# Weight conversion through one PSUM bank, and attention products issued straight behind the scores

## The chip, the cores and the metric

One core of one Trainium2 chip runs the whole program. The metric is the device time of one execution in microseconds (us), as the median of several. Five engines work side by side, each through its own instruction stream in order: TensorE (PE in the profile, its weight loads PEld), VectorE (DVE), ScalarE (ACT), GpSimd (POOL), and SyncE (SP), which issues the DMAs. They meet only at semaphores.

## The reference

Two layers follow each other. The first is attention with 8 batches, 8 heads, 576 positions and head size 64, in which each row of scores keeps only its 32 largest:

```
scores = q @ k.T / 8
kth    = 32nd largest of each row
scores = where(scores >= kth, scores, -1e9)
attn   = exp(scores - max); attn = attn / (sum + 1e-9)
x      = attn @ v                       # heads side by side: 576 x 512 for each batch
```

The second is a gated feed-forward layer with d_ff = 1024:

```
h    = relu(x @ w_in)                   # 576 x 1024
conv = cw[0]*h[s-1] + cw[1]*h[s] + cw[2]*h[s+1]
out  = (h * sigmoid(conv)) @ w_out      # 576 x 512
```

The weights `w_in`, `conv_w` and `w_out` arrive as 64-bit floats. [...]

## The kernel before

**Attention.** Two heads form a pair (`pc`); a batch has four pairs, and the program has 32 of them in order. The rows of a pair are cut into 9 tiles, j = 0 to 8: for j = 0 to 7 an even and the odd tile behind it are 128 query rows of the one head and of the other, and j = 8 holds the last 64 rows of both. That makes 288 tiles. `iteration(it)` runs once for each, and in every iteration each engine gets the work of several tiles that stand at different stages:

- PE (line order in the iteration): four transposes of the weighted row e of a tile (L306, into the bank `pt`), a budget of feed-forward matmuls (`run_units`, L804: expand L404 into `me`, contract L554 into `mc`), the transpose of the tail (L319), the scores of a new tile pair (`scores`, L811, only in iterations whose new tile has an even j), and the attention product (`av`, L813) of an earlier pair.
- ACT: the sign of each score against the threshold (L268), the copy of a score tile out of PSUM (`evacuate`, L228), the copy of the transposes (L311), the copy of a finished product (`av_out`, L348), the exponential of a tile (L280), and then tanh (L465), relu (L418), casts (L531) and tail copies (L323) of the feed-forward part.
- DVE: seven partial top-8 (L235) woven with their merges (L255, L257), `below` (L283), `select` (L287, called hot in the profile), the gates of the feed-forward layer (L473), and last `weigh` (L293), which multiplies the exponential with the mask.
- POOL: the weight conversion's arithmetic, the convolution, and `flip` (L273).

For PE, DVE, ACT and POOL the order is the order in which this code issues the instructions; no scheduler moves them. `weigh` needs the exponential of the iteration before, the next exponential overwrites its only buffer and so waits for `weigh`, and the transposes of the next iteration need its result.

**PSUM.** The scores lie in one tile of three banks, `s_ps`. An even tile is read from columns 0 to 575 (bank 0 and the start of bank 1), an odd one from 960 to 1535 (the end of bank 1 and bank 2). The two scores matmuls (L219, 64 rows of the array each) fill banks 0 and 2; a third with all 128 rows (`ends`, L222) fills the two 64-column pieces at the edges of bank 1. The attention product writes to the middle of the same bank 1 (`corner`, L121). Dependencies between engines are kept by bank, so whoever reads or writes any column of bank 1 waits for whoever used that bank on another engine before.

**When the attention product comes.** The pair whose second tile is transposed in one iteration is put on a list, and `av` runs in the next. That next iteration has an odd new tile, and so no scores. Its result is copied by L348 one iteration later, which is one with scores.

**Weight conversion.** 33 blocks (one of 24 columns, then 32 of 128 x 256) are converted, one per iteration: seven while the pipeline fills, before the first `weigh`, and then one in each of the next 26 iterations. One block takes three DVE instructions: L150 cuts the 16-bit exponent field out of the raw words, L151 the high mantissa, L161 puts the sign into the power. ACT makes the power from the field (L155) and two floats from the mantissa words (L156, L157); POOL multiplies and splits (L166 to L172). All these operands lie in SBUF. The feed-forward layer of a batch starts when its attention is done.

Of the kernel before, what the change touches and what calls it, by code (L numbers as in the profile page):

```python
# [13 lines left out]
BF16 = mybir.dt.bfloat16  # L14
U16 = mybir.dt.uint16
# [48 lines left out]
def attend_and_feed(ctx: ExitStack, tc: tile.TileContext, q, k, v, weights, out, shared, finish=None):  # L64
# [53 lines left out]
    def bank(name):  # L118
        return ps.tile([P, BANK], F32, name=name, tag=name, bufs=1)
# [6 lines left out]
    class Convert:  # L126
# [5 lines left out]
        def load(self):  # L132
            i = Convert.count
            Convert.count += 1
            if not scratch:
                scratch.append(moe.tile([P, 4 * SPB, WB], F32, name="scratch", tag="split"))
            self.at = i % SPB * 4
            tag = ("x_hi", "x_lo")[i % 2]
            self.raw = xp.tile([P, self.src.shape[-1], 2], U32, name="raw64", tag=tag)[0:self.n]
            nc.sync.dma_start(out=self.raw.rearrange("a c t -> a (c t)"), in_=self.src.bitcast(U32))  # L140
# [2 lines left out]
            return scratch[0][0:self.n, self.at + i, 0:self.raw.shape[1]]  # L143

        def split(self):
            exponent, self.mantissa, self.rest = (self.tmp(i) for i in range(3))
            n = exponent.shape[1]
            self.field, self.power = exponent.bitcast(U16)[:, 0:n], exponent.bitcast(BF16)[:, n:2 * n]
            self.top = self.raw.rearrange("a c t -> a (c t)").bitcast(U16).rearrange("a (c t) -> a c t", t=4)[:, :, 3]
            yield lambda: nc.vector.tensor_scalar(self.field, self.top, 0x7FF0, None, ALU.bitwise_and)  # L150
            yield lambda: nc.vector.tensor_scalar(self.mantissa.bitcast(U32), self.raw[:, :, 1], 0xFFFFF, 0x100000,  # L151
                                                  ALU.bitwise_and, ALU.bitwise_or)

        def act(self):
            nc.scalar.activation(out=self.power, in_=self.field, func=AF.Exp, scale=math.log(2.0) / 16, bias=offset)  # L155
            nc.scalar.activation(out=self.mantissa, in_=self.mantissa.bitcast(U32), func=AF.Copy, scale=2.0 ** -20)  # L156
            nc.scalar.activation(out=self.rest, in_=self.raw[:, :, 0], func=AF.Copy, scale=2.0 ** -52)  # L157

        def sign(self):
            power = self.power.bitcast(U16)  # L160
            yield lambda: nc.vector.scalar_tensor_tensor(out=power, in0=self.top, scalar=0x8000, in1=power,  # L161
                                                         op0=ALU.bitwise_and, op1=ALU.bitwise_or)

        def pool(self):
            x = self.mantissa
# [40 lines left out]
    def scores(t):  # L206
        kx, qx = t.pc.nat["k"], t.pc.nat["q"]
        i = t.j // 2
        rows_of = [slice(h * D, (h + 1) * D) for h in range(2)]
        if t.j == 2 * NI:  # L210
            for to, n in ((0, MAIN), (MAIN, TAIL)):
                for h, d in enumerate(rows_of):
                    at = (to + TAIL * h) % S
                    nc.tensor.matmul(s_ps[rows_of[1 - h], to:to + n], lhsT=qx[d, 0:TAIL], rhs=kx[d, at:at + n],  # L214
                                     start=True, stop=True)
        elif t.j % 2 == 0:
            at = slice(TAIL + i * P, TAIL + (i + 1) * P)
            for h, d in enumerate(rows_of):
                nc.tensor.matmul(s_ps[:, 2 * h * BANK:(2 * h + 1) * BANK], lhsT=qx[d, at],  # L219
                                 rhs=kx[d, h * TAIL:h * TAIL + MAIN], start=True, stop=True)  # L220
            ends = s_ps[:, BANK:2 * BANK].rearrange("p (a c) -> p a c", c=TAIL)[:, 0:BANK // TAIL:BANK // TAIL - 1]
            nc.tensor.matmul(ends, lhsT=qx[:, at], rhs=kx[:, S:S + 2 * TAIL], start=True, stop=True)  # L222

    def evacuate(t):
        t.row = rows[:, t.n % XBUFS]
# [488 lines left out]
    def iteration(it):  # L714
        nonlocal av_next, out_next, rec_next
        n = it + 3
        state.it = it
        pre, tA, tB, tC = (tiles.get(i) for i in (it + 2, it, it - 1, it - 2))
        tX, tD, tE = tiles.get(it - 3), tiles.get(it - 4), tiles.get(it - 5)

        for lane in lanes:
            while lane.finished and lane.finished[0].room():
                lane.waiting -= 1
                lane.finished.popleft().emit()
        while split_next() and it > NT + 4:
            pass
        avs, av_next = av_next, []
        both = tE is not None and (tE.j % 2 == 1 or tE.j == 2 * NI)
        if tE is not None:
            transposes(tE)  # L730
        if n < NT:
            pc, j = work[n]
            if j == 0 and n and pcs.index(pc) + 1 < len(pcs):
                fetch(pcs[pcs.index(pc) + 1])
            t = Box()
            t.n, t.j, t.pc = n, j, pc
            t.st = pc.steps[j // 2]
            tiles[n] = t

        if tC is not None and not exact:  # L740
            sides(tC)
        if pre is not None:
            evacuate(pre)
        if tE is not None:
            transposed(tE)
        outs, out_next = out_next, []
        for st in outs:
            av_out(st)
            if st.i == NI:
                norm_wait.append((it + NORM_LAG, st.pc))  # L750

        if exact:
            a_ops, b_ops = [], list(exact_ops(tB)) if tB is not None else []
        else:
            a_ops = list(chunk_ops(tA)) if tA is not None else []
            b_ops = list(cand_ops(tB)) if tB is not None else []
        pool_used = CONV_COST * len(dved)
        convert_pool()
        c_first, c_last = convert_dve()
        for i in range(max(7, len(a_ops), len(b_ops))):  # L760
            if i < len(a_ops):
                a_ops[i]()
            for op in c_first[i:i + 1]:
                op()
            if tD is not None and not exact:
                if i == BELOW_AT:
                    below(tD)
                if i == BELOW_AT + 2:
                    select(tD)
            if i < len(b_ops):  # L770
                b_ops[i]()
        for op in c_last:
            op()
        while gates:
            gates.popleft().gate()
        recs, rec_next = rec_next, []
        if tD is not None:
            weigh(tD)
            if tD.j == NBLK - 1:
                inverses(tD.pc)  # L780
                rec_next.append(tD.pc)

        if tX is not None:
            expo(tX)
        if tD is not None and not exact:
            edges(tD)
        if tD is not None and tD.j == 0:
            load_v(tD.pc)
        while tanh_now:
            e = tanh_now.popleft()  # L790
            e.tanh()
            if e.pooled():
                pool_tasks.append((it + 1, 2.01 * e.n / S + 0.1, e.gate_pool))
            else:
                gates.append(e)
        tanh_now.extend(tanh_next)
        tanh_next.clear()
        convert_act()
        if norm_wait and norm_wait[0][0] <= it:
            pc = norm_wait.pop(0)[1]  # L800
            for task in reversed(normalise(pc) + [(0, 0.0, lambda pc=pc: start(pc))]):
                pool_tasks.appendleft(task)
        state.credit = min(state.credit + (FEED if it < NT + 5 else 9.0), PE_CAP)
        state.credit -= max(state.credit, 0.0) - run_units(max(state.credit, 0.0))  # L804
        for pc in recs:
            norms(pc)
        if both:
            state.credit += run_units(0.0, lanes[0])
            tails(tE.st)
        if n < NT:  # L810
            scores(tiles[n])  # L811
        for st in avs:
            av(st)  # L813
        out_next.extend(avs)
        if tE is not None:
            if both:
                tailed(tE.st)
                av_next.append(tE.st)
            del tiles[tE.n]

        state.pool = max(min(state.pool, 0.0) + POOL_BUDGET - pool_used, 0.0) if tC is not None else 9.0
        flipped = tC is None or exact
        while pool_tasks and state.pool > 0.2 and pool_tasks[0][0] <= it:
            if not flipped and state.pool < FLIP_AT:
                flip(tC)
                flipped = True
            _, c, fn = pool_tasks.popleft()
            fn()
            state.pool -= c
        if not flipped:  # L830
            flip(tC)
# [134 lines left out]
```

## Time and profile before

| | |
|---|---|
| time, median of 3 runs | 1152.47 us (1152.42 to 1154.94) |
| the profiled execution | 1155.28 us, span in the trace 1153.4 us |
| busy share of the span | DVE 92%, PE 90%, ACT 86%, POOL 78% |
| chain that ended last | DVE 45%, PE 42%, ACT 11% |

The program has three parts. Up to about 160 us the weights are converted beside the attention. From about 290 to 1044 us attention and feed-forward run side by side and repeat. The last 109 us hold feed-forward alone, where PE works and the others wait. A share of busy time over the whole span mixes these, so the rows below are taken from single stretches. "Idle before, and releaser" names the instruction that, by its semaphore, let a waiting one go.

### The profile page before, as it was taken

The numbers are of one execution on the slowest core, as the hardware profiler recorded it, in microseconds if no ns is written. First come the engines' busy times: TensorE is split into PE (matmuls) and PEld (weight loads), VectorE is DVE, ScalarE is ACT, GpSimd is POOL, SyncE is SP. The second block draws the span as 40 slices with busy tenths as digits, with TensorE's granted clock in tenths as the row PEclk, the third lists the DMA queues.
The fourth block names the chain that finished last, engine by engine and source line by source line (L and its number), as shares of the span: only waits on it lengthen the run. The fifth ranks groups of instructions, "written<-read, shape, count | busy, mean of one in ns | idle before, by whom it ended". The sixth has DMA issues, their size and how long they took to land.

```text
span 1153.4 us, 27267 instructions
## 1 busy us (share of the span) xinstructions
PE 1035.3 (90%) x7970; PEld 767.3 (67%) x7970; DVE 1064.5 (92%) x5834; ACT 996.5 (86%) x2343; POOL 895.6 (78%) x1078
## 2 busy tenths in 40 slices
PE   3665676788999999999999999999999999999997
PEld 1443444566767776777777767777777677777896
DVE  7999999999999999999999999999999999998651
ACT  5777868899999999999999999999999999998442
POOL 6788864688979888898978887987978897898300
PEclk9967659999999999999999999999999999999999
DMA  7221101111111111111111112121211011110001
GB/s 242 79 68 41 46 17 40 46 38 44 55 54 56 56 46 65 46 55 56 49 38 44 56 45 64 47 64 46 64 55 56 24 38 59 55 33 21 31 28 40
DMA packets 51694, 60.75 MB, mean 53 GB/s; under 512 B 9776, under 2 KB 30544, under 8 KB 51536
## 3 DMA queue, kind: packets, MB, share of 16 engines
q1 hardware_dynamic: 51536, 58.91, 16.0%
q8 instruction: 66, 1.08, 0.4%
q14 instruction: 92, 0.75, 0.2%
HBM read 49.31 MB, written 9.58 MB: 51 GB/s over the span
## 4 chain that ended last, share of the span: by engine, by line
DVE 45%; PE 42%; ACT 11%; issue 1%; DMA 0%; SPq 0%; POOL 0%; ACTq 0%; POOLq 0%
DVE cand L235 13%; DVE e L293 9%; PE mc L554 9%; PE me L404 8%; DVE z L283 7%; PE s_ps L337 6%; PE s_ps L219 5%; PE pt L306 5%; DVE cand L257 3%; ACT weights_ps L280 2%; DVE scratch L161 2%; DVE rows L255 2%; PE s_ps L222 2%; DVE hot L287 2%; PE weights_ps L554 2%; PE s_ps L214 2%
## 5 line engine op out<-in xcount | busy, mean ns | idle before, releaser
L273 POOL TENSOR_TENSOR z<-rows,side 128x579 f32<-128x579 f32 x288 | 347.4, 1206 | 143.0 <-ACT side L268 122.5
L235 DVE MAX8 cand<-rows 128x8 f32<-128x82 f32 (+1 forms) x2016 | 451.0, 238 | 0.0
L280 ACT ACTIVATE weights_ps<-rows,z 128x576 f32<-128x576 f32 x288 | 219.8, 763 | 42.4 <-DVE e L293 31.5
L293 DVE SCALAR_TENSOR_TENSOR e<-rows,kth,weights_ps 128x576 f32<-128x576 f32 x288 | 230.1, 799 | 0.3
L268 ACT ACTIVATE side<-rows 128x576 bf16<-128x576 f32 x288 | 224.2, 778 | 0.8 <-DVE rows L255 0.5
L404 PE MATMUL me<-x_hi,wi 128*128 128x322 f32 (+1 forms) x928 | 218.6, 308 | 1.2 <-ACT g L418 1.2
L283 DVE MAX8 z<-z 128x8 f32<-128x576 f32 x288 | 213.7, 742 | 0.0
L228 ACT COPY rows<-s_ps 128x576 f32<-128x576 f32 x288 | 183.0, 635 | 33.7 <-PE s_ps L340 20.3
L219 PE MATMUL s_ps<-k,q 64*128 64x512 f32 x512 | 155.1, 684 | 59.6 <-ACT xt L348 44.9
L306 PE MATMUL pt<-ident,e 128*128 128x128 f32 x1152 | 191.8, 292 | 8.9 <-DVE e L293 8.9
L337 PE MATMUL s_ps<-pT,vn 128*64 128x128 f32 (+1 forms) x2560 | 171.2, 279 | 17.7 <-ACT rows L228 17.7
L554 PE MATMUL mc<-wo,split 128*128 128x512 f32 x684 | 186.5, 406 | 0.0
L337 PEld LDWEIGHTS s_ps<-pT,vn 128*64 128x64 f32 x2560 | 134.3, 143 | 54.7 <-ACT rows L228 28.0
L306 PEld LDWEIGHTS pt<-ident,e 128*128 128x128 f32 x1152 | 135.3, 148 | 35.3 <-issue 20.1
L404 PEld LDWEIGHTS me<-x_hi,wi 128*128 128x128 f32 x928 | 157.1, 189 | 2.4 <-ACT g L418 2.1
L311 ACT COPY pT<-pt 128x512 f32<-128x512 f32 x256 | 152.0, 594 | 3.4 <-PE pt L306 3.2
L404 PE MATMUL me<-x_lo,wi 128*128 128x258 f32 (+1 forms) x464 | 138.5, 299 | 0.0
L554 PEld LDWEIGHTS mc<-wo,split 128*128 128x128 f32 x684 | 120.1, 189 | 19.6 <-issue 0.2
L437 POOL TENSOR_SCALAR t<-g,cr 128x256 f32<-128x256 f32 (+1 forms) x222 | 113.6, 512 | 0.0
L222 PEld LDWEIGHTS s_ps<-k,q 128*128 128x128 f32 x256 | 40.9, 201 | 105.6 <-issue 105.6
L255 DVE MAX8 rows<-cand 128x8 f32<-128x21 f32 x576 | 108.9, 189 | 0.2 <-issue 0.2
L219 PEld LDWEIGHTS s_ps<-k,q 64*128 64x128 f32 x512 | 40.6, 194 | 91.2 <-ACT xt L348 58.8
(121 smaller groups left out, 1865.6 us busy)
## 6 DMA issues: line engine op xcount, KB each, us to landing
k<-in_k_dram SPq DMA_DIRECT2D x32, 352.0 KB
q<-in_q_dram SPq DMA_DIRECT2D x32, 288.0 KB
vn<-in_v_main_dram SPq DMA_DIRECT2D x32, 256.0 KB
rb<-row SPq DMA_DIRECT2D x64, 128.0 KB
out_dram<-o SPq DMA_DIRECT2D x24, 256.0 KB
raw<-in_w_in_dram SPq DMA_DIRECT2D x16, 256.0 KB
raw<-in_w_out_dram SPq DMA_DIRECT2D x16, 256.0 KB
vt<-in_v_tail_dram SPq DMA_DIRECT2D x32, 64.0 KB
```

Of the source, the lines that this page charges most:

```text
L219: nc.tensor.matmul(s_ps[:, 2 * h * BANK:(2 * h + 1) * BANK], lhsT=qx[d, at], rhs=kx[d, h * TAIL:h * TAIL + MAIN], start=True, stop=True)
L228: nc.scalar.copy(out=x, in_=s_ps[:, at:at + S])
L235: yield lambda c=c, at=at, n=n: nc.vector.max(out=t.cand[:, c:8 * CHUNKS:CHUNKS], in_=t.x[:, at:at + n])
L268: nc.scalar.activation(out=t.side[:, 2:S + 2], in_=t.x, func=AF.Sign, scale=-OVER, bias=t.row[:, 7:8], accum_out=t.cnt)
L273: nc.gpsimd.tensor_tensor(t.z[:, 8:S + 11], t.row[:, 6:S + 9], t.side, ALU.mult)
L280: nc.scalar.activation(out=e_ps, in_=t.x, func=AF.Exp, scale=scale, bias=t.shift)
L283: nc.vector.max(out=t.z[:, 0:8], in_=t.z[:, 10:S + 10])
L293: nc.vector.scalar_tensor_tensor(out=t.e, in0=t.x, scalar=kth[:, t.n:t.n + 1], in1=e_ps, op0=ALU.is_ge, op1=ALU.mult, accum_out=t.pc.sums[ ...
L306: nc.tensor.transpose(tp[:, i * P:(i + 1) * P], t.e[:, o + i * P:o + (i + 1) * P], ident)
L337: nc.tensor.matmul(a[r, 0:w], lhsT=st.pc.vn[:, h, i], rhs=st.pT[:, h if st.i < NI else 1 - h, i, 0:w], start=(i == 0), stop=False)
L404: nc.tensor.matmul(mm[:, 0:w], lhsT=wt, rhs=xx, start=(n == 0), stop=(n == len(ops) - 1))
L554: nc.tensor.matmul(mm[0:m], lhsT=x[:, i], rhs=wo[:, e, f], start=start, stop=stop)
```

## The change

There are three edits.

1. In the weight conversion the exponent field and the high mantissa now go to two halves of one PSUM bank (`mc`, which the feed-forward layer uses later) and are taken with 32-bit operations. ACT copies the power (bf16) into that bank as 32-bit floats (one instruction more per block), and the sign instruction reads one operand from there. The three DVE instructions stand in other places of the iteration: sign first, behind the fifth partial top-8, then the field, then the mantissa.
2. Attention products are held. In an iteration with an odd new tile the list is kept, except for the fourth pair of rows, so that the first three of the five products of each pair of heads run one iteration later, straight behind scores.
3. The edge matmul `ends` stands in front of the two scores matmuls.

```diff
@@ load, split, act, sign
             if not scratch:
                 scratch.append(moe.tile([P, 4 * SPB, WB], F32, name="scratch", tag="split"))
+                mc = bank("mc")
+                scratch.extend((mc[:, 0:WB], mc[:, WB:2 * WB]))
...
-            yield lambda: nc.vector.tensor_scalar(self.field, self.top, 0x7FF0, None, ALU.bitwise_and)
-            yield lambda: nc.vector.tensor_scalar(self.mantissa.bitcast(U32), self.raw[:, :, 1], 0xFFFFF, 0x100000,
+            self.power, self.mantissa, self.rest = (self.tmp(i) for i in range(3))
+            self.two = self.power.bitcast(BF16)[:, 0:self.power.shape[1]]
+            self.field, self.bits = (x[0:self.n, 0:self.raw.shape[1]] for x in scratch[1:])
+            self.top = self.raw[:, :, 1]
+            yield lambda: nc.vector.tensor_scalar(self.field.bitcast(U32), self.top, 0x7FF00000, None, ALU.bitwise_and)
+            yield lambda: nc.vector.tensor_scalar(self.bits.bitcast(U32), self.top, 0xFFFFF, 0x100000,
                                                   ALU.bitwise_and, ALU.bitwise_or)
...
-            nc.scalar.activation(out=self.power, in_=self.field, func=AF.Exp, scale=math.log(2.0) / 16, bias=offset)
-            nc.scalar.activation(out=self.mantissa, in_=self.mantissa.bitcast(U32), func=AF.Copy, scale=2.0 ** -20)
+            nc.scalar.activation(out=self.two, in_=self.field.bitcast(U32), func=AF.Exp, scale=math.log(2.0) / 2 ** 20,
+                                 bias=offset)
+            nc.scalar.copy(out=self.field, in_=self.two)
+            nc.scalar.activation(out=self.mantissa, in_=self.bits.bitcast(U32), func=AF.Copy, scale=2.0 ** -20)
...
-            yield lambda: nc.vector.scalar_tensor_tensor(out=power, in0=self.top, scalar=0x8000, in1=power,
-                                                         op0=ALU.bitwise_and, op1=ALU.bitwise_or)
+            yield lambda: nc.vector.scalar_tensor_tensor(out=self.power.bitcast(U32), in0=self.top, scalar=0x80000000,
+                                                         in1=self.field.bitcast(U32), op0=ALU.bitwise_and,
+                                                         op1=ALU.bitwise_or)
@@ scores
             at = slice(TAIL + i * P, TAIL + (i + 1) * P)
+            ends = s_ps[:, BANK:2 * BANK].rearrange("p (a c) -> p a c", c=TAIL)[:, 0:BANK // TAIL:BANK // TAIL - 1]
+            nc.tensor.matmul(ends, lhsT=qx[:, at], rhs=kx[:, S:S + 2 * TAIL], start=True, stop=True)
             for h, d in enumerate(rows_of):
...
-            nc.tensor.matmul(ends, lhsT=qx[:, at], rhs=kx[:, S:S + 2 * TAIL], start=True, stop=True)
@@ iteration
-        avs, av_next = av_next, []
+        held = n < NT and work[n][1] % 2
+        avs = [st for st in av_next if not held or st.i == NI - 1]
+        av_next = [st for st in av_next if st not in avs]
...
-            for op in c_first[i:i + 1]:
+            for op in (c_last + c_first)[i - 4:i - 3] if i > 3 else ():
...
-        for op in c_last:
-            op()
```

On PE, two iterations in the feed-forward part of the kernel before: `e` is the weighted row that is transposed, `split` and `wo` the operands of the contract matmuls, `pT`, `pTt`, `vn`, `vt` those of the attention product.

```order
L306 MATMUL pt<-ident,e_8343 128x128 x4
L554 MATMUL mc<-wo,split 128x512 x9
L337 MATMUL s_ps<-pT,vn 64x128 x8
L340 MATMUL s_ps<-pTt,vt 64x128 x2
L306 MATMUL pt<-ident,e_8343 128x128 x4
L554 MATMUL mc<-wo,split 128x512 x6
L319 MATMUL me<-ident,e_8343 128x128
L219 MATMUL s_ps<-k,q 128x512 x2
L222 MATMUL s_ps<-k,q 128x2x64
L306 MATMUL pt<-ident,e_8454 128x128 x4
```

The same place of the changed kernel (its line numbers are 4 to 6 higher):

```order
L310 MATMUL pt<-ident,e_8377 128x128 x4
L558 MATMUL mc<-wo,split 128x512 x9
L310 MATMUL pt<-ident,e_8377 128x128 x4
L558 MATMUL mc<-wo,split 128x512 x6
L323 MATMUL me<-ident,e_8377 128x128
L223 MATMUL s_ps<-k,q 128x2x64
L225 MATMUL s_ps<-k,q 128x512 x2
L341 MATMUL s_ps<-pT,vn 64x128 x8
L344 MATMUL s_ps<-pTt,vt 64x128 x2
L310 MATMUL pt<-ident,e_8488 128x128 x4
```

The ten matmuls of the product went from the first iteration, in front of the second one's transposes, to the end of the second, behind the scores; the edge matmul went in front of the scores. All feed-forward matmuls stand in the iterations in which they stood.

On DVE, the second half of one iteration during the conversion, before (`raw` is a block's 64-bit words, `scratch` its SBUF buffer), with the semaphores that an instruction waits for:

```order
L235 MAX cand<-rows 128x8
L257 MATCH_REPLACE cand<-second,cand 128x35 [waits DVE_49]
L235 MAX cand<-rows 128x8
L287 SCALAR_TENSOR_TENSOR hot,kth<-weights_ps,cnt,z 128x10 [waits Activation_49]
L255 MAX rows<-cand 128x8 [waits DVE_49]
L235 MAX cand<-rows 128x8 x2
L161 SCALAR_TENSOR_TENSOR scratch<-raw_352,scratch 128x256 [waits Activation_49]
L293 SCALAR_TENSOR_TENSOR e_992,sums<-rows,kth,weights_ps 128x576 [waits DVE_49,PE_49]
```

And in the changed kernel:

```order
L239 MAX cand<-rows 128x8
L261 MATCH_REPLACE cand<-second,cand 128x35 [waits DVE_49]
L239 MAX cand<-rows 128x8
L164 SCALAR_TENSOR_TENSOR scratch<-raw_316,mc 128x256 [waits Activation_49]
L291 SCALAR_TENSOR_TENSOR hot,kth<-weights_ps,cnt,z 128x10
L259 MAX rows<-cand 128x8 [waits DVE_49]
L239 MAX cand<-rows 128x8
L152 TENSOR_SCALAR mc<-raw_361 128x256 [waits DMAHW3_49,DVE_49]
L239 MAX cand<-rows 128x8
L153 TENSOR_SCALAR mc<-raw_361 128x256 [waits DVE_49]
L297 SCALAR_TENSOR_TENSOR e_899,sums<-rows,kth,weights_ps 128x576
```

The sign went from the end of the iteration to its middle, ahead of `select`, and its wait is for the third of the four ACT instructions of its block (the copy of the mantissa out of `mc`); the two others came from the iteration's start to behind it.

## Rows read from the trace of the kernel before

**Rows 1.** Busy time by stretch: length, busy by engine (instructions), granted clock, DMA, GB/s.

```profile
29.00:145.00 116.00, 73.75 (x430) 46.38 (x430) 115.86 (x514) 87.04 (x214) 94.63 (x121) 0.76 0.18 58
290.00:1044.00 754.00, 737.00 (x5955) 550.49 (x5954) 729.69 (x4238) 714.79 (x1676) 646.39 (x765) 1.00 0.16 51
```

**Rows 2.** Groups of DVE instructions by form: busy us, mean ns, idle before.

```profile
L161 DVE SCALAR_TENSOR_TENSOR scratch<-raw,scratch 128x256 uint16<-128x256 uint16 x32 | 31.2, 975 | 0.0
...
L473 DVE SCALAR_TENSOR_TENSOR g<-weights_ps,g 128x256 f32<-128x256 f32 x49 | 19.9, 407 | 0.0
...
L150 DVE TENSOR_SCALAR scratch<-raw 128x256 uint16<-128x256 uint16 x32 | 17.5, 546 | 1.2 <-DMA raw<-in_w_in_dram 1.2
...
L151 DVE TENSOR_SCALAR scratch<-raw 128x256 uint32<-128x256 uint32 x32 | 13.6, 424 | 0.0
```

**Rows 3.** Timeline (start us, duration us): the sign instruction in the conversion, and POOL.

```profile
29.12 0.60 DVE L161 SCALAR_TENSOR_TENSOR scratch<-raw,scratch 128x256 uint16<-128x256 uint16 x1
...
98.32 1.35 DVE L161 SCALAR_TENSOR_TENSOR scratch<-raw,scratch 128x256 uint16<-128x256 uint16 x1
99.34 0.91 POOL L166 TENSOR_TENSOR scratch<-scratch 128x256 f32<-128x256 f32 x1
...
158.33 0.40 DVE L161 SCALAR_TENSOR_TENSOR scratch<-raw,scratch 128x256 uint16<-128x256 uint16 x1
```

**Rows 4.** Timeline of ACT in one iteration of the conversion.

```profile
100.49 0.74 ACT L280 ACTIVATE weights_ps<-rows,z 128x576 f32<-128x576 f32 x1 [1.65 <-DVE e L293]
101.17 0.49 ACT L155 ACTIVATE scratch<-scratch,offset 128x256 bf16<-128x256 uint16 x1
101.57 0.40 ACT L156 ACTIVATE scratch<-scratch 128x256 f32<-128x256 uint32 x1
...
103.48 0.57 ACT L311 COPY pT<-pt 128x512 f32<-128x512 f32 x1
```

**Rows 5.** Timeline of DVE in one iteration without conversion, gate or stall.

```profile
849.88 0.08 DVE L293 DVE_READ_ACCUMULATOR e<-rows,kth,weights_ps 128x1 f32 x1
...
851.78 0.20 DVE L287 SCALAR_TENSOR_TENSOR hot<-weights_ps,cnt,z 128x10 f32<-128x10 f32 x1
...
853.06 0.08 DVE L293 DVE_READ_ACCUMULATOR e<-rows,kth,weights_ps 128x1 f32 x1
```

**Rows 6.** Timeline of PE during the conversion, in a stretch of low granted clock.

```profile
93.83 1.55 PE L219 MATMUL s_ps<-k,q 64*128 64x512 f32 x4 [2.99 <-ACT xt L348]
...
95.90 1.06 PE L306 MATMUL pt<-ident,e 128*128 128x128 f32 x4
98.41 1.98 PE L337 MATMUL s_ps<-pT,vn 128*64 128x128 f32 x16 [1.44 <-ACT rows L228]
...
100.74 1.12 PE L306 MATMUL pt<-ident,e 128*128 128x128 f32 x4
```

**Rows 7.** Waits of DVE from 290 to 1044 us: total us, times, longest.

```profile
DVE hot L287 <- ACT weights_ps L465: 17.2, 28, 1.7
```

**Rows 8.** Waits of ACT in the same stretch.

```profile
ACT rows L228 <- PE s_ps L340: 13.2, 25, 1.2
...
ACT rows L228 <- PE s_ps L222: 6.3, 22, 0.5
```

**Rows 9.** Waits of PE in the same stretch.

```profile
PE s_ps L219 <- ACT xt L348: 10.2, 13, 1.4
```

**Rows 10.** Timeline of PE in that stretch, at full clock.

```profile
847.33 1.13 PE L219 MATMUL s_ps<-k,q 64*128 64x512 f32 x4
...
848.71 0.60 PE L306 MATMUL pt<-ident,e 128*128 128x128 f32 x4
...
850.66 0.27 PE L319 MATMUL me<-ident,e 128*64 128x128 f32 x1
850.86 1.09 PE L337 MATMUL s_ps<-pT,vn 128*64 128x128 f32 x16
...
852.10 0.66 PE L306 MATMUL pt<-ident,e 128*128 128x128 f32 x4
```

More of the change, by code (lines that the diff above doesn't have):

```diff
@@ L145, in split @@
         def split(self):
[L146 to L149, printed above, removed]
-            yield lambda: nc.vector.tensor_scalar(self.field, self.top, 0x7FF0, None, ALU.bitwise_and)
-            yield lambda: nc.vector.tensor_scalar(self.mantissa.bitcast(U32), self.raw[:, :, 1], 0xFFFFF, 0x100000,
+            self.power, self.mantissa, self.rest = (self.tmp(i) for i in range(3))
@@ L157, in act @@
             nc.scalar.activation(out=self.rest, in_=self.raw[:, :, 0], func=AF.Copy, scale=2.0 ** -52)
         def sign(self):
-            power = self.power.bitcast(U16)
-            yield lambda: nc.vector.scalar_tensor_tensor(out=power, in0=self.top, scalar=0x8000, in1=power,
-                                                         op0=ALU.bitwise_and, op1=ALU.bitwise_or)
+            yield lambda: nc.vector.scalar_tensor_tensor(out=self.power.bitcast(U32), in0=self.top, scalar=0x80000000,
+                                                         in1=self.field.bitcast(U32), op0=ALU.bitwise_and,
+                                                         op1=ALU.bitwise_or)
@@ L220, in scores @@
                                  rhs=kx[d, h * TAIL:h * TAIL + MAIN], start=True, stop=True)
-            ends = s_ps[:, BANK:2 * BANK].rearrange("p (a c) -> p a c", c=TAIL)[:, 0:BANK // TAIL:BANK // TAIL - 1]
-            nc.tensor.matmul(ends, lhsT=qx[:, at], rhs=kx[:, S:S + 2 * TAIL], start=True, stop=True)
     def evacuate(t):
```

## The prediction, made before the changed kernel ran

> **What bounds the kernel now.** I read busy time by stretch first, since the page's shares mix three parts. From 29 to 145 us, beside the weight conversion, DVE is busy for 115.86 of 116 us and nobody else for more than 95 [rows 1]: that stretch is DVE's. From 290 to 1044 us three engines are nearly full: PE 737.00, DVE 729.69 and ACT 714.79 of 754 us [rows 1]. Here the waits decide, so I read them next. DVE's idle 24.3 us are mostly `select` held by ACT's tanh into the bank that it reads, 17.2 us in 28 waits [rows 7]. ACT is late because it has waited itself: 13.2 us in its copy of a score tile until the attention product was done (L340), and 6.3 us in the same copy until the edge matmul was done [rows 8]. PE waits back, 10.2 us in front of the scores for ACT's copy of a finished product [rows 9]. Each of the two sends the other its bank 1 in every iteration, and DVE pays when ACT is late. The last 109 us are PE's feed-forward matmuls; the change leaves them as they are.
>
> **Conversion.** Removed are three DVE instructions per block with means of 0.975, 0.546 and 0.424 us [rows 2]. The sign shows what makes them slow: beside POOL's reading it takes 1.35 us, in POOL's gap 0.40 [rows 3]. Added are a sign that reads one operand from PSUM, and two 32-bit instructions that write to PSUM. For the sign I take 0.41, the mean of a DVE instruction of its kind and size with one PSUM operand [rows 2]; its bounds are 0.40 and the 0.975 of today. For the other two I take 0.42 each, the mean of the 32-bit form of today [rows 2], since no row shows a raw word going to PSUM; the 16-bit form bounds them at 0.55 and nothing says that they get quicker. So DVE's work per block falls from 1.95 to 1.25 us.
>
> Today an iteration takes 4.97 us: from 29.12 to 158.33 us are 26 of them [rows 3]. One without conversion takes 3.18 [rows 5], so 1.79 of the 1.95 show and 0.15 overlap with neighbours. With the same overlap the new one is 3.18 + 1.25 - 0.15 = 4.28 us for DVE alone. But the sign now stands at the place of `select`, 1.90 us behind the start of the last piece of `weigh` and so 1.82 behind its end [rows 5], and must wait for ACT. ACT starts its exponential when `weigh` ends, then follow 0.68 us to the field's exponential, 0.49 for that (whole, as the new copy needs its result), and two copies of 256 columns at 0.40 each [rows 4]: 1.97, and with some 0.05 for each of four hand-overs (my estimate) 2.2 us. The sign stalls for about 0.37, and the iteration takes 4.65.
>
> That the sign waits for the copy of the mantissa, which it does not read, is in the instruction order, and it agrees with `select` today, which waits for a tanh into other columns of its bank [rows 7]. The Trainium skill (PSUM — Partial Sum Buffer, "PSUM bank collisions raise a hardware error") says that PSUM must be guarded by bank and not by address. By it the wait stays; if address alone counted, the sign would be ready 0.45 us earlier, at its place, and the iteration would take 4.28. The trace is on the rule's side.
>
> While PE's clock is granted at its lower level (0.76 on the mean of the stretch [rows 1] is about half of the time at 1.2 GHz) the held product costs something. Scores with edge take 2.07 us there and a product 2.33 [rows 6], now in one piece. ACT's copy that frees the bank ends about 3.7 us after its exponential began (2.2, and the 1.5 that lie today between the end of L156 and the next L311 [rows 4]), so the product ends at 8.1, the transposes behind it 1.06 later [rows 6], and their copy at 9.8, where ACT wants its second next exponential at 9.3. That is 0.5 us late, for three pairs of every nine iterations: 0.2 per iteration at the low level. I take 4.75 us for the mean of both levels, so 26 x 0.22 = 5.7 us less. The seven blocks ahead of the first `weigh` I cost at nothing: the inputs' transfers cover them. Bounds: 26 x (4.97 - 4.28) = 18 us less, and 3 us more if every iteration pays the low clock's 0.5 (5.1 us).
>
> **Held products.** The product's place matters through bank 1. Today the odd tile's copy comes behind a product (13.2 us of waiting), and scores come behind the copy of that product [rows 8, 9]. Now the product comes behind scores and its result is read an iteration later, so the odd tile's copy follows scores that were done a whole iteration before: that wait goes, save in the iterations of the fourth and fifth product, which are not moved. The scores now wait for the tile's copy and no longer for the transposes' copy and the product's. What comes next: the even tile's copy, which waited for the edge matmul for 6.3 us, now waits for the product, 1.24 us of PE work later (850.86 to 852.10 [rows 10]). But PE reaches the scores 1.24 us earlier too, since the product no longer stands in the iteration before. So I leave that wait at 6.3.
>
> PE's work is unchanged: 1.38 us for scores with edge, 1.24 for a product [rows 10], as many as before. Of the order within them I expect nothing: a product starts 0.20 us after the tail's transpose [rows 10], so its entry costs between nothing and 0.2, and the scores behind the edge matmul may cost as much or save it. Three moved products of each of 32 pairs of heads make 96, some 70 of them in this stretch by its share of the time ahead of the last 109 us; that is at most 14 us of PE's time either way. The Trainium skill (TensorEngine Tiling (Array Packing), "Key Properties") says that a change of tiling mode drains TensorE. By it the run from the edge (128 rows) over the scores (64 rows) and the product (64 columns) back to the transposes changes mode three times, where scores and product apart changed it four times, so by it PE would gain some of those 14 us; no row here measures it.
>
> So ACT can gain up to 13.2 us, and DVE, which only loses its 24.3 idle us, up to 24 with PE's help. ACT's lateness reaches DVE only where it exceeds the slack ahead of `select`, and where an iteration carries much of the feed-forward part's ACT work it stays late without any wait. I take half of DVE's idle time: 12 us less, bounds 0 and 24. Outside of this stretch I count nothing.
>
> **Sum.** 5.7 + 12 is 18 us off the profiled execution's 1155.28, which is 1137.5. The runs shown have a median 2.8 us below that execution, so 1152.47 - 18 gives 1134.5 us.
>
> **Rivals.**
> - Both steps in full: sign not held back, DVE full from end to end: 18 + 24 = 42 us less, 1110. For it speaks that DVE's rows show no other reason to stall; against it that ACT has 714.79 of 754 us to do anyway [rows 1].
> - ACT's lateness is its own: heavy iterations and not PE's waits make the 17.2 us [rows 7]. Then the held products bring some 2 us and the conversion its 5.7: 1145. For it: ACT's waits number 25 and 22 against DVE's 28, but each is 0.5 us on the mean [rows 8], often within slack.
> - Slower: PE does not reach the scores earlier, since it stands in front of them until ACT has copied the odd tile. Then the product ends 1.24 us later for ACT. In the 22 places where ACT waits for the edge matmul already [rows 8] that is 22 x 1.24 = 27 us, the low clock adds 26 x 0.13 = 3, and against it stands the 13.2 that goes: 17 us more, 1169. It decides from the point where the scores' wait, now 10.2 us in 13 places [rows 9], becomes the rule. PE is at 98% and mostly behind ACT, which speaks against it.
> - It does not do what it says: the wait for a product's copy is only renamed, as j = 0 and j = 8 keep it, and the sign's stall eats the conversion's gain: within 0.3%.
>
> **How the numbers follow.** Forecast (1124 to 1143) 0.53; both in full 0.13; ACT's own lateness 0.20; slower 0.08; renamed 0.06. The median of this kernel can tell about 0.3% (3.5 us) from no change. The second rival at 1145 is still 0.65% faster. So faster 0.86, same 0.06, slower 0.08. The range reaches up to the second rival and a little past it, and down half the way to the first: 1117 to 1149.
>
> **What would show it.** Right: the sign at 0.40 to 0.45 us whatever POOL does, with a wait of 0.3 to 0.5 us in front of it for ACT's copy of the mantissa; iterations of 4.6 to 4.9 us up to 160 us; no wait of the odd tile's copy for a product from 290 to 1044 us, and DVE idle for about 12 us less there. Wrong: signs or PSUM writes above 0.55 us; waits of the even tile's copy for L344 well above 6.3 us in total, or waits of the edge matmul for that copy in most pairs; DVE's idle time in the long stretch still above 20 us.

## The result and the profile after

| | before | after |
|---|---|---|
| time, median of 4 runs each | 1153.51 us (1152.42 to 1154.94) | 1168.55 us (1165.88 to 1169.12) |
| the profiled execution, its span | 1155.28, 1153.4 us | 1165.88, 1164.4 us |
| chain that ended last | DVE 45%, PE 42%, ACT 11% | PE 51%, ACT 23%, DVE 21% |

The change makes the kernel slower: ratio 1.0125, interval 1.0104 to 1.0147. The forecast was 1134.5 us; the rival with a chance of 0.08 had 1169. The chain has moved from DVE to PE and ACT.

For the place of the loss I count from one start of `weigh` to another; a pair of heads has nine. "First weigh" is where the first one starts, "end" runs from pair 31 to the last row of the timeline, the issue of the last DMA. The table has the two kernels and the first four experiments (us, each from one profiled execution). Pairs 7 to 30 repeat closely between kernels with the same attention part (754.5 and 754.6; 768.1 and 768.2), so that differences there can be read to some tenths of a microsecond; the pairs ahead of them vary by more.

| | first weigh | pairs 0 to 2 | pairs 3 to 6 | pairs 7 to 30 | end |
|---|---|---|---|---|---|
| before | 29.6 | 132.6 | 122.4 | 754.5 | 108.9 |
| after | 28.0 | 128.6 | 124.7 | 768.1 | 109.3 |
| conversion alone | 28.0 | 121.6 | 119.0 | 754.6 | 109.3 |
| attention part alone | 30.0 | 132.6 | 126.5 | 768.2 | 110.0 |
| hold alone | 29.4 | 132.2 | 121.7 | 774.1 | 110.1 |
| edge first alone | 29.5 | 132.5 | 124.6 | 753.9 | 108.6 |

In the changed kernel, busy time by stretch answers [rows 1] (columns as there):

```profile
29.00:145.00 116.00, 71.16 (x419) 43.69 (x421) 103.55 (x538) 101.65 (x247) 96.51 (x128) 0.77 0.18 56
290.00:1044.00 754.00, 725.06 (x5855) 548.40 (x5854) 718.29 (x4163) 703.61 (x1648) 637.11 (x752) 1.00 0.16 50
```

DVE is no longer full in the first stretch (103.55 of 116 us, 115.86 before). In the second, all four engines do less in the same 754 us. Instructions got no longer on the mean (PE 0.124 us, DVE 0.172, ACT 0.427, in both kernels): everything waits more. The groups of the three conversion instructions by form answer [rows 2] (busy us, mean ns, idle before):

```profile
L164 DVE SCALAR_TENSOR_TENSOR scratch<-raw,mc 128x256 uint32<-128x256 uint32 x32 | 13.5, 421 | 15.5 <-ACT scratch L160 15.4
L153 DVE TENSOR_SCALAR mc<-raw 128x256 uint32<-128x256 uint32 x32 | 13.3, 415 | 0.0
L152 DVE TENSOR_SCALAR mc<-raw 128x256 uint32<-128x256 uint32 x32 | 13.3, 415 | 0.0
```

They are as quick as forecast. The waits from 290 to 1044 us answer [rows 7 to 9] (total us, times, longest):

```profile
ACT rows L232 <- PE s_ps L344: 32.7, 50, 2.2
...
DVE hot L291 <- ACT weights_ps L469: 22.8, 30, 2.1
PE s_ps L223 <- ACT rows L232: 17.9, 23, 2.1
...
DVE hot L291 <- ACT weights_ps L284: 10.5, 18, 1.3
```

ACT's copy of a score tile waits for the product 50 times, 32.7 us, where it waited 13.2 for the product and 6.3 for the edge matmul. PE's edge matmul now waits for that copy, 17.9 us in 23 places, where PE waited 10.2 for the copy of a product. DVE's `select` pays: 33.3 us by the two rows, and 21.3 before, the 17.2 of [rows 7] and these 4.1:

```profile
DVE hot L287 <- ACT weights_ps L280: 4.1, 6, 1.1
```

One of the two worst places shows the order of events (pair 24 in the table's count). First the kernel before (start us, duration us; PE has the last product of the odd iteration, then the even tile's scores and edge):

```profile
837.45 0.39 PE L340 MATMUL s_ps<-pTt,vt 128*64 128x128 f32 x4
...
838.54 0.62 ACT L228 COPY rows<-s_ps 128x576 f32<-128x576 f32 x1
...
839.86 1.13 PE L219 MATMUL s_ps<-k,q 64*128 64x512 f32 x4 [1.32 <-ACT xt L348]
...
840.92 0.49 PE L222 MATMUL s_ps<-k,q 128*128 128x128 f32 x2
...
841.44 0.64 ACT L228 COPY rows<-s_ps 128x576 f32<-128x576 f32 x1
```

The same place in the changed kernel:

```profile
842.83 0.27 PE L323 MATMUL me<-ident,e 128*128 128x128 f32 x1
...
844.36 0.62 ACT L232 COPY rows<-s_ps 128x576 f32<-128x576 f32 x1
...
845.03 0.53 PE L223 MATMUL s_ps<-k,q 128*128 128x128 f32 x2 [1.92 <-ACT rows L232]
...
845.49 2.08 PE L225 MATMUL s_ps<-k,q 64*128 64x512 f32 x4
...
847.49 1.69 PE L341 MATMUL s_ps<-pT,vn 128*64 128x128 f32 x16
...
849.01 0.39 PE L344 MATMUL s_ps<-pTt,vt 128*64 128x128 f32 x4
...
849.45 0.64 ACT L232 COPY rows<-s_ps 128x576 f32<-128x576 f32 x1 [2.18 <-PE s_ps L344]
...
851.46 0.23 DVE L291 SCALAR_TENSOR_TENSOR hot<-weights_ps,cnt,z 128x10 f32<-128x10 f32 x1 [0.92 <-ACT weights_ps L284]
```

Before, the product was done when ACT came to the odd tile's copy, and of PE's matmuls only scores and edge lay between that copy and the even tile's, behind a wait of 1.32 us for ACT's copy of the product. Now PE has finished its transposes at 843.1 and stands for 1.92 us until ACT has copied the odd tile; then edge, scores and product run in one piece; ACT waits 2.18 us for the end of it, and `select` 0.92 for ACT. Here the clock adds to it: scores took 2.08 us instead of 1.13.

### The profile page after: what moved, and what is told of

Same layout as the page of the kernel before. It is cut to its first block, busy times and chain, and to the rows that moved or that the text cites. A ratio compares the mean times of both kernels' runs of the same rounds, so it can differ in the third digit from the quotient of the medians.

```text
span 1164.4 us, 27252 instructions
## 1 busy us (share of the span) xinstructions
PE 1034.7 (89%) x7970; PEld 771.6 (66%) x7970; DVE 1045.8 (90%) x5834; ACT 1010.0 (87%) x2376; POOL 892.0 (77%) x1078
## 4 chain that ended last, share of the span: by engine, by line
PE 51%; ACT 23%; DVE 21%; issue 3%; DMA 1%; SPq 0%; POOL 0%; ACTq 0%
PE me L408 9%; PE s_ps L341 9%; PE mc L558 9%; PE s_ps L225 8%; DVE cand L239 6%; PE pt L310 6%; DVE e L297 5%; ACT weights_ps L284 5%; ACT side L272 4%; ACT rows L232 4%; DVE z L287 3%; PE s_ps L223 3%; PE s_ps L218 2%; PE s_ps L344 2%; PE weights_ps L558 2%
## 5 line engine op out<-in xcount | busy, mean ns | idle before, releaser
L239 DVE MAX8 cand<-rows 128x8 f32<-128x82 f32 (+1 forms) x2016 | 456.4, 239 | 0.1
L310 PE MATMUL pt<-ident,e 128*128 128x128 f32 x1152 | 188.9, 287 | 22.6 <-ACT pT L315 9.1
L310 PEld LDWEIGHTS pt<-ident,e 128*128 128x128 f32 x1152 | 128.3, 143 | 88.6 <-issue 43.2
L225 PE MATMUL s_ps<-k,q 64*128 64x512 f32 x512 | 161.0, 708 | 0.0
L558 PEld LDWEIGHTS mc<-wo,split 128*128 128x128 f32 x684 | 120.1, 189 | 20.2 <-ACT o L574 0.8
L223 PE MATMUL s_ps<-k,q 128*128 128x128 f32 x256 | 61.3, 324 | 76.4 <-ACT rows L232 65.7
```

What stands on the lines that cost most here:

```text
L239: yield lambda c=c, at=at, n=n: nc.vector.max(out=t.cand[:, c:8 * CHUNKS:CHUNKS], in_=t.x[:, at:at + n])
L310: nc.tensor.transpose(tp[:, i * P:(i + 1) * P], t.e[:, o + i * P:o + (i + 1) * P], ident)
L558: nc.tensor.matmul(mm[0:m], lhsT=x[:, i], rhs=wo[:, e, f], start=start, stop=stop)
```

## The experiments

Theory A: held, the product lies in the loop from ACT's copy of the odd tile over PE to ACT's copy of the even tile, both through bank 1. B: the edge matmul in front makes the scores late. C: the new conversion disturbs the attention.

**Conversion alone**: the changed kernel with its attention part taken back (edge behind the scores again, and no hold).

```
...
-        held = n < NT and work[n][1] % 2
-        avs = [st for st in av_next if not held or st.i == NI - 1]
-        av_next = [st for st in av_next if st not in avs]
+        avs, av_next = av_next, []
```

> The conversion through the PSUM bank alone, attention order as before. Theory A (held products close a longer ring between PE and ACT through bank 1) and theory B (the edge matmul in front makes the scores start later) both put the whole loss into the attention edits, so here the kernel is faster by the 3 to 4 us that the first weigh rows of pair 7 show in the changed kernel (281.2 against 284.7 us): 1149 to 1151 us. Theory C (the conversion shifts the phase of the engines and so harms the long stretch, or its bank mc does) says no gain or slower: 1153 to 1165, with the loss between pairs 7 and 31.

Measured: 1139.63 us, ratio 0.9882 (0.9846 to 0.9918): a gain of 14 us. It lies ahead of pair 7 (11.0 us in pairs 0 to 2, 3.4 in pairs 3 to 6, 1.6 ahead of the first `weigh`); pairs 7 to 30 take 754.6 us as before. C falls for the long stretch, and the conversion was worth more than I gave it. Not all of the 3.4 us need be the conversion's, which is over before pair 3: PE's granted clock in pairs 3 to 6 was 0.94 before and 0.98 here.

**Attention part alone**: the kernel before with the two attention hunks of the diff, edge first and hold.

> Both attention edits, conversion as before. Theories A and B: slower than before by what the long stretch lost in the changed kernel (768.1 against 754.4 us from pair 7 to pair 31), and a little more in the conversion stretch, where the lower clock makes the longer ring cost most: 1165 to 1171 us. Theory C: within 3 us of before.

Measured: 1174.33 us, ratio 1.0164 (1.0132 to 1.0197), a little above what A gave. Pairs 7 to 30 take 768.2, the changed kernel's 768.1.

**Hold alone**: the kernel before with the hold; the edge matmul stays behind the scores.

```
-        avs, av_next = av_next, []
+        held = n < NT and work[n][1] % 2
+        avs = [st for st in av_next if not held or st.i == NI - 1]
+        av_next = [st for st in av_next if st not in avs]
```

> Products held as in the changed kernel, the edge matmul behind the scores as before. Theory A: nearly the whole loss, 1162 to 1171 us; ACT's copy of the even tile waits for the product for 25 us or more between 290 and 1050 us. Theory B: about 1153.

Measured: 1176.13 us, ratio 1.0195 (1.0162 to 1.0228). The time is above A's 1162 to 1171: the hold alone loses 19.6 us in pairs 7 to 30, and the edge in front gives 6 of them back there. Over the whole run the two versions with the hold differ by 1.8 us, and their intervals overlap.

**Edge first alone**: only the two lines of `ends` moved.

> The edge matmul in front of the scores alone, products as before. Theory A: within 2 us of before, perhaps 1 to 3 us faster, since the entry into the scores is 0.09 us shorter (0.11 from the tail's transpose to the edge matmul, 0.20 to the scores). Theory B: 1160 to 1168, with the wait for the copy in front of the edge matmul well above the 14 us that the scores wait before.

Measured: 1153.0 us, ratio 0.9991 (0.997 to 1.0012). B falls. ACT's waits for the product from 290 to 1044 us, in this run and then in the attention part alone, which differs from it by the hold:

```profile
ACT rows L228 <- PE s_ps L340: 14.8, 26, 1.4
```

```profile
ACT rows L228 <- PE s_ps L340: 32.2, 49, 2.2
```

That leaves the hold, and two readings of it: each held product costs the same, or only the third of a pair, which lands in front of the iterations with the fourth and fifth product.

**Two held / only the third held**, both with edge first and the old conversion:

```
-        avs = [st for st in av_next if not held or st.i == NI - 1]
+        avs = [st for st in av_next if not held or st.i >= NI - 2]    # two held
+        avs = [st for st in av_next if not held or st.i != NI - 2]    # third held
```

> The attention part of the change (edge product in front) without the conversion, but only the first two of the three products of a pair are held to the following iteration; the third stands where it stood before. Theory 1 (each held product makes the loop from ACT's copy of the odd tile over TensorE to ACT's copy of the even tile longer by the same amount): two thirds of the loss stay, pairs 7 to 30 take 754 + 9 = 763 us, the whole about 1167. Theory 2 (only the third costs, since it is moved right in front of the iterations with the fourth and fifth products and the normalisation, where nothing is left to take up a delay; delays of the first two are taken up by the iterations behind them): pairs 7 to 30 take 755 to 758 us, the whole 1154 to 1159.

> The complement: edge product in front, and only the third product of a pair is held, the first two stand where they stood before. Theory 1 (same price for each held product): one third of the loss, pairs 7 to 30 take 754 + 4.6 = 759 us, the whole about 1160. Theory 2 (only the third costs): nearly the whole loss, 764 to 768 us in pairs 7 to 30, the whole 1165 to 1172.

Measured: two held 1168.41 us, ratio 1.0108 (1.0074 to 1.0143), pairs 7 to 30 in 764.1 us; the third held 1158.51, ratio 1.0037 (1.002 to 1.0055), 759.8 us. Against 753.9 without a hold that is 10.2 and 5.9, together about the 14.3 of all three: on the mean each held product costs 0.20 to 0.25 us, whichever it is. The first reading holds. PE's clock could be a rival here: among these pairs it is at the lower level for a short time in one place with two held and with the third held, in two places with all three, and nowhere with edge first alone. In the pairs without such a place a held product costs 0.15 us (all three), 0.14 (two) and 0.17 (the third), so the reading stands without it. The wait follows: ACT's copies of the even tiles 2, 4 and 6 of a pair wait 1.7 us in all without a hold, 17.1 with two held, 6.7 with the third, 24.6 with all.

**Short products**, free and held: if it is the product's length in the loop, a shorter one must cost less. Both runs leave out four of the ten matmuls of each of these products.

```
-        for i in range(NI + 1):
+        for i in [0, 1, NI] if st.i < NI - 1 else range(NI + 1):
```

> The base for the next run: old conversion, edge product in front of the scores, products where they stood before, but each of the first three products of a pair leaves out four of its ten matmuls (the third and fourth block of both heads), so that it takes about 0.74 us of TensorE instead of 1.24. Every theory expects pairs 7 to 30 between 742 and 754 us (the copy of the odd tile waits less for a shorter product, 14.8 us in all at full length).

> The same short products, and now the three are held. Theory 1 (what the hold costs is the length of the product, which lies between ACT's copy of the odd tile and ACT's copy of the even one; the full product ends only about 0.4 us later than the edge product did before): shorter by 0.5 us, it ends no later than the edge product did, so pairs 7 to 30 take the time of the run without the hold, within 4 us to either side (the hold costs 14 us at full length). Theory 2 (the hold costs by its place, whatever its length: TensorE stands at the edge product until ACT has copied the odd tile, and the transposes and feed-forward products behind start late): 10 to 14 us more than without the hold, as at full length.

Measured: free 1144.56 us, ratio 0.9905 (0.9881 to 0.993), pairs 7 to 30 in 746.5 us; held 1151.33, ratio 0.996 (0.9943 to 0.9978), 753.3 us. The hold costs 6.7 us instead of 14.3: neither the "within 4" of length alone nor the "10 to 14" of place alone. ACT's waits for a product, free and then held:

```profile
ACT rows L228 <- PE s_ps L340: 7.2, 15, 1.2
```

```profile
ACT rows L228 <- PE s_ps L340: 14.3, 19, 2.1
```

Pair 24 holds 3.5 of the 6.7, and there scores run for 2.08 us, the low clock again. But the low clock blurs the sum both ways. The held run also has it in pairs 7 and 28, and the free run in pairs 19 and 28, where the held run is 1.2 and 1.1 us quicker. The 20 pairs in which none of the four runs has it lose 3.5 us here and 7.5 with the whole product. So the length makes about half of the price. The rest, which I put down to PE's standing still ahead of the edge matmul, is not shown; no run takes it away.

**Conversion with a late sign**: conversion alone, but the sign two slots later and the other two operations behind the loop, to let ACT's copies finish.

```
-            for op in (c_last + c_first)[i - 4:i - 3] if i > 3 else ():
+            for op in c_last if i == 6 else ():
...
+        for op in c_first:
+            op()
```

> The new conversion on PSUM operands in the kernel before, products not held, but the sign operation of a block is placed two slots later in its iteration and the field and mantissa operations behind the loop, so that the sign's wait for ACT's mantissa copy (9.2 us in 31 blocks of the run with the conversion alone) should go. Theory 1 (VectorE is what ends an iteration of the conversion stretch, so the waits were part of the price): most of the 9 us comes back, some 1131 to 1135, iterations near 4.2 us. Theory 2 (with the conversion alone, the iteration of 4.45 us is set by the loop from ACT's row copies over TensorE back to ACT, VectorE's wait lies beside it): 1138 to 1141, iterations stay at 4.4 to 4.5 us, and the wait only moves to VectorE's next operation.

Measured: 1137.92 us, ratio 0.9848 (0.9817 to 0.9879); against conversion alone pairs 0 to 2 gain 1.5 us and pairs 3 to 6 lose 1.4. Busy time from 29 to 145 us of conversion alone, and then of this run:

```profile
29.00:145.00 116.00, 74.40 (x470) 47.18 (x470) 108.89 (x565) 106.66 (x262) 101.58 (x134) 0.80 0.18 56
```

```profile
29.00:145.00 116.00, 72.34 (x470) 46.30 (x470) 112.73 (x575) 107.55 (x263) 102.46 (x135) 0.79 0.18 58
```

The sign's wait goes as meant (6.9 us to 1.2 in this stretch, 9.2 to 2.3 in the whole run), DVE does ten instructions more in the stretch, and the time as a whole does not move beyond the intervals. Theory 2's time came out (120.1 / 27 = 4.45 us for an iteration of pairs 0 to 2). Its reason did not: no wait took the place of the one removed, and what ends an iteration is DVE, at 112.73 of 116 us, with ACT at 107.55 behind it. With the conversion alone the chain that ended last went a round in this stretch: from `weigh` over ACT's exponential and three of its conversion instructions (39.5% together) to the sign and back to `weigh`. With the late sign it stays on DVE for over 70% of the stretch.

**Conversion and edge first, no hold**: the change without its middle part.

> The change without its hold: new conversion, edge product in front of the scores, products where they stood before. If the two other parts add up (conversion -14, edge first -1 to 0): 1138 to 1141, pairs 7 to 30 near 754 us. If the conversion stretch gains only because the old order of scores and edge product left TensorE room there: above 1145.

Measured: 1140.43 us, ratio 0.9881 (0.9848 to 0.9915); pairs 7 to 30 in 754.0. The two add up. The changed kernel differs from this one by the hold alone and takes 1168.55 us: the hold costs 28 us there, twice what the conversion gains. All three versions with the new conversion and no hold beat both kernels; which of the three is best can't be told, as their intervals overlap.

## Why the prediction was wrong

**The step that failed** is in "Held products": "But PE reaches the scores 1.24 us earlier too, since the product no longer stands in the iteration before. So I leave that wait at 6.3." I moved the work and forgot what frees it. The edge matmul writes bank 1, so it cannot start before ACT has copied the odd tile out of it, however early PE is there. On the mean of the iterations with j = 4 (pairs 7 to 30, counted from the end of the last `weigh`) PE began scores at 4.36 us before and begins the edge at 3.44 now: 0.92 earlier, not 1.24. The edge ended at 5.91, the product ends at 6.31: what ACT waits for is 0.40 later. For j = 6 it is 0.43 later, for j = 2 only 0.03 (PE comes 0.76 and 1.18 us earlier). At j = 2 and 4 ACT itself is free for the copy 0.3 and 0.2 us earlier than before, now that its odd copies no longer wait, and finds the product still running. The waits of the even tiles 2, 4 and 6 grow from 4.0 to 25.0 us, and the 12 us that I booked as gain of DVE came out as loss: `select` waits 33.3 us instead of 21.3. The copy reads none of the columns that the product writes. The Trainium skill (PSUM — Partial Sum Buffer, "PSUM bank collisions raise a hardware error") says to guard PSUM by bank and quadrant, or more simply by bank, and not by address. The kernel's waits follow the Trainium skill in this: 40 of the 50 waits for L344 stand in front of such copies. I had used the rule for the sign and not here.

**The 13.2 us of odd tiles were too large a stake.** Of that wait [rows 8] only 5.6 us belong to the tiles 3, 5 and 7 and 1.5 to tile 1; they go to 0.0, as forecast. 6.1 us belong to tile 8, which waits behind the fifth product; it stays, at 7.6. I had excepted these iterations in words, and left them in the number.

**Why 21 us more of waiting cost 13.6.** Against the 21 us stand the 7.1 of odd tiles that went. And not every wait is passed on. No iteration of the long stretch is shorter than 3.17 us, with DVE at work throughout. Of the 216 iterations of pairs 7 to 30, 107 were there before (3.22 or less) and 92 are now. 46 iterations became longer by over 0.1 us, 18.7 us in all; 19 became shorter, 5.2 in all. I read this as slack of ACT, in which a late copy costs nothing.

**The rival that came out** had the place and the mechanism: PE "stands in front of them until ACT has copied the odd tile". Its sum agrees partly by luck. It priced 22 places at 1.24 us; it is about 0.2 us on the mean for each of the 72 held products of that stretch. It also gave the conversion no gain, which was 14 us, and the low clock 3, where the conversion's stretch lost far more:

**Conversion.** The instructions came as forecast (0.421, 0.415, 0.415 us against 0.41 and 0.42). For the last two that is partly luck: the 0.424 of [rows 2] is a mean of 19 blocks at 0.28 to 0.33 us and 13 at 0.52 to 0.60, while with the result in PSUM every block takes 0.41 to 0.43. The stall behind ACT's mantissa copy came as forecast too with the conversion alone: 9.2 us in 31 blocks are 0.30 each, 0.37 was forecast (in the changed kernel 16.2 us, 0.52 each). Sized wrongly was the sum: with the conversion alone an iteration takes 121.6 / 27 = 4.50 us, not 4.65, and DVE's 108.89 busy us with 6.9 of that stall fill the 116. That leaves no room for a price of the low clock (0.80 there), for which I had added 0.10. The changed kernel's 4.76 (128.6 / 27) match the forecast 4.75, but as a gain of 0.41 and a loss of 0.26 per iteration. The loss is the hold: against conversion with edge first (121.1 and 118.8 us) it takes 7.5 us in pairs 0 to 2 and 5.9 in pairs 3 to 6, there with the clock at 0.95 against 0.97. The old conversion hid it, because there DVE was full and ACT waited anyway: attention alone leaves pairs 0 to 2 at 132.6. The sign of conversion alone, on DVE:

```profile
94.93 0.42 DVE L164 SCALAR_TENSOR_TENSOR scratch<-raw,mc 128x256 uint32<-128x256 uint32 x1 [0.19 <-ACT scratch L160]
...
99.38 0.42 DVE L164 SCALAR_TENSOR_TENSOR scratch<-raw,mc 128x256 uint32<-128x256 uint32 x1 [0.19 <-ACT scratch L160]
```

and of the changed kernel:

```profile
97.41 0.42 DVE L164 SCALAR_TENSOR_TENSOR scratch<-raw,mc 128x256 uint32<-128x256 uint32 x1 [1.50 <-ACT scratch L160]
...
101.86 0.42 DVE L164 SCALAR_TENSOR_TENSOR scratch<-raw,mc 128x256 uint32<-128x256 uint32 x1 [0.19 <-ACT scratch L160]
```

The first pair stands 4.45 us apart with the same short wait, block after block. In the second, ACT comes late after a held product and the sign waits 1.50 us.

**The rest.** PE's work in the long stretch was forecast unchanged within 14 us. Edge first moves that stretch by 0.6 us without a hold and by 5.9 with one, 0.08 us for each of the 72 products. The Trainium skill (TensorEngine Tiling (Array Packing), "Key Properties") says that a change of tiling mode drains TensorE. Only with the hold does edge first save such a change, one of four; the runs agree with that but do not separate it from the rest of the loop. The end and the bounds of the conversion (18 less to 3 more) held.

## What to carry to other kernels

When work moves from one iteration to the next, draw the loop through the buffer that both engines share, and sum what lies between its two copies; the start of the moved work is set by what frees the buffer, not by when its engine has time. A wait that is to disappear must be split by the iterations that have it before it is booked as a gain. A part that gains and a part that loses can hide in a mean that fits, so each is timed alone.

## What the runs showed of the hardware

At the place shown above PE waited 1.92 us and then ran at the low clock. The stretch of the changed kernel ahead of the end of that wait, and the one behind it (columns as in [rows 1]):

```profile
842.00:845.00 3.00, 1.10 (x7) 0.53 (x5) 2.02 (x13) 2.97 (x8) 2.92 (x4) 1.00 0.01 3
845.00:849.40 4.40, 4.37 (x27) 2.54 (x28) 4.40 (x28) 2.16 (x5) 3.24 (x4) 0.61 0.01 4
```

0.61 is mostly the lower level of 1.2 GHz; scores then take 2.08 us. In the long stretch, which I had read as full clock throughout, this happens to two of 95 groups of scores in the changed kernel (at 845.5 and 975.8 us) and to none of 96 before, where the same place waited 1.32 us and stayed at 1.00. The iterations at these two places are 1.02 and 1.12 us longer than before, the pairs 24 and 28 around them 3.9 together, so that the other 22 pairs lose 9.7 of the 13.6 us without it.

The length of one wait does not settle it. With the hold alone PE waits 1.92 us at the same place, and the clock stays up:

```profile
854.38 1.13 PE L219 MATMUL s_ps<-k,q 64*128 64x512 f32 x4 [1.92 <-ACT rows L228]
```

```profile
854.40:858.80 4.40, 4.40 (x40) 3.35 (x41) 4.40 (x28) 3.70 (x9) 3.18 (x4) 1.00 0.03 7
```

Pair 24 is 2.3 us longer than before there all the same. That run loses 19.6 us in pairs 7 to 30 and has the lower level in one place only, from 730.8 us on, 1.6 us behind a wait of 1.47 us. The short free products, without any hold, have it in two places. Why the clock fell at one of these waits and not at another is open.

The sign operation with one operand in PSUM takes 0.41 to 0.42 us in all 32 blocks, with POOL at work beside it in 30 of them, where the form with both operands in SBUF went from 0.40 to 1.35 [rows 3]. POOL hardly gains: its first product of a block takes 0.73 us, 0.86 before, but its second 0.73, 0.67 before (means from 29 to 145 us).
